# New order lists for tiles 3 to 8 of a fused attention and ReGLU kernel, with six of eight corner clears per tile on GpSimd

## The chip, the cores and the metric

The kernel runs on one core of a Trainium2 chip. The metric is device time in microseconds (us) of one execution, the median of several runs. A core has a matrix engine (TensorE, PE in the profile, with its weight loads as PEld), and VectorE (DVE), ScalarE (ACT), GpSimd (POOL) and SyncE (SP). Each has its own list of instructions and executes it in order; between engines, semaphores make a reader wait for its writer. DMA transfers are issued from the lists of SP, ACT and POOL. SBUF is the on-chip memory; PSUM holds matmul results in eight banks.

## The reference

The kernel must compute block-causal attention, and then a gated feed-forward layer on its output:

```python
# q, k, v: (8 batches, 8 heads, 576 rows, 64), block = 64
scores = scale * np.matmul(q, k.transpose(0, 1, 3, 2))
mask = block_i >= block_j
attn = softmax(np.where(mask, scores, -1e9))
attn_out = np.matmul(attn, v)
x = attn_out.transpose(0, 2, 1, 3).reshape(8 * 576, 512)
# w_gate, w_val: (512, 1536), w_out: (1536, 512)
gate = np.maximum(x @ w_gate, 0.0)
val = x @ w_val
out = gate * val @ w_out          # (4608, 512), float32
```

## The kernel before

**Tiles.** The 4608 output rows are made in nine tiles of 512. Tile j, for j from 0 to 7, holds the first 512 rows of batch j; tile 8 holds the last 64 rows of all eight batches. While the feed-forward layer of tile j is computed, the attention of batch j+1 runs in its gaps, and q, k and v of batch j+2 are loaded. So tiles 0 to 6 carry attention work, and tiles 7 and 8 do not.

**Two ways of ordering.** All engines run under a manual schedule: the order in which the program calls the operations is the order of each engine's list. Tiles 0 to 2 come from a generator of feed-forward steps (`ffn_gen`), between which actions of the attention are called when a count of steps reaches their due time (the table `AT`). Tiles 3 to 8 come from `program(j)`, which executes a written list of tokens one by one: `ORDER_3_6` for tiles 3, 4, 5 and 6, `ORDER_7` and `ORDER_8` for the last two.

**Tokens of the attention.** (The next batch is `up`.)
- `A` followed by a digit: a visit, the score matmuls of 128 query rows (L611). `E1s`, `E1f`, `E1t`, `E1u`: its four exponentials on ACT (L616, L623). `K` and `k`: the last 64 keys (L640) and their exponential (L649).
- `C` and two digits: the corners. The exponentials of a visit also fill blocks that the mask excludes; they are set to zero (L1526 on DVE, L1529 on POOL) before the products read them.
- `V`: products of the probabilities with v for half of the heads (L759, L773), into one PSUM bank. `N`: division by the row sums (reciprocal L696, products L698 and L705, on DVE).
- `T`: the result of a visit is transposed to `xT` by a DMA that SP issues (L842), the input of the next tile's feed-forward layer.
- `l` and `w`: loads of q and k, and of v, issued by POOL (L489). `d0` to `d3`: DMA transposes of q, k and their tails, issued by SP (L499, L504, L506).

**Tokens of the feed-forward layer.** The hidden dimension is cut into 12 chunks of 128. Chunks 0, 1, 8 and 9 of tiles 3 to 6 are computed plainly: `g` and `v` are the matmuls (L1322), `r` the relu on ACT (L1317), `h` the product of the gate and the value (L1445, DVE). The other chunks go in pairs (pairs 1, 2, 3 and 5 in tiles 3 to 6, all six in tiles 7 and 8), each by Strassen's method: seven products of half-size blocks in place of eight. `p15` is product 5 of pair 1 (L1348). The parts of a pair are joined by copies on ACT (`a` L1371, `b` L1374, `l` L1389) and additions (`s` L1377, `m` L1382, `y` L1393, `z` L1396), and `H` and `L` (L1401, L1415) multiply them with the relu and write the hidden activations `hT`. The output product is done by seven products too: `M` and a digit, six tokens each (L1033), whose operands are sums of `hT` blocks (`s` and four digits, L992); tokens `o` add the results (L1080, with ACT's copies L1085, L1092 and L1095) and `S` stores them (L886 for tile 8). `X` and `Y` are sums of `xT` blocks (L1154), `P` is the last store of the previous tile, and `U` (in tile 6 only) are sums of weight blocks that tiles 7 and 8 need (L950).

**Banks and engines.** Several tables go with the lists: `SLOTS` says which of the buffers of a kind each new tile of that kind takes (the PSUM banks `sc` and `ffnp`, and the SBUF buffers `ob` and `gate_sb`), `PAIR_BANK` and `AV_BANK` which banks a pair's products and the products `V` use, and `ON_POOL` which tokens run on POOL instead of DVE. A token that is named with its tile and in `ON_POOL` runs on POOL, such as `31H` for `p1H` in tile 3. A buffer comes free when its last reader has finished. So the position of a token in the list decides both when an engine gets to it and how long its bank is held.

The corner tokens do this (L1476 to L1482):

```python
elif k == "C":
    i, c = map(int, of)
    corners(
        4 * up + i,
        zero_pool if f"{i}C" in ON_POOL else zero_dve,
        (((0, 512),), ((896, 128),))[c],
    )
```

No name of that form is in `ON_POOL`, so all eight clears of tiles 3 to 6 run on DVE. The line in the changed kernel differs, as the diff shows.

Of the kernel before, what the change touches and what calls it, by code (L numbers as in the profile page):

```python
# [17 lines left out]
def kernel(  # L18
# [27 lines left out]
            "010101010101010010101010101010101010101010101010101010101001110010100110"  # L46
            "100111001010011010011100101001101001110010100110100110100101"
# [3 lines left out]
            "201021102101020120120120121201202101202101202101210210201102220201101202"  # L51
            "001201202112000202112102022102102011022202011012020012012021120002021121"
            "0202210210122001201200121012012"
        ),
        "ob": (
            "043210432104310420312142324014203124304232410421302431423240142031243042"
            "324104210324103140231403"
# [5 lines left out]
    }  # L63
    ORDER_3_6 = """
        A0 E0t X1 X3 X4 X6 Y4 g0 X7 E0u E0s C01 E0f g0 K g0*2 r0 k g1*2 v0*2 C00 l0 l1
        l2 v0 p15 v0 h0 p15 p1a g1*2 V00 U02 N00 r1 P V01 N01 p12*2 p1b p1s p13 l3 w0
        p13 p1r p11 v1*2 p11 l4 l5 p1m p14 p16*2 p1y d0 p14 p1l v1 U01 U06 U42 l6 l7 l8
        d1 d2 A1 E1u v1 h1 p17*2 p32 E1t E1s E1f p25*2 p32 g8 p1z p1L C11 p22*2 g8*2
        p35*2 C10 s0101 p1H s0112 p2a p23*2 p2b p24 p21 g8 p21 p24 p3b p2r p26 s0012 l9
        l10 d3 w1 p3a p3s s0001 p26 p2s p2m p2y p2H p33*2 p31*2 p3m p2l p27*2 p2z p3r  # L70
        p36*2 p3y r8 p34*2 p3l V11 N11 A2 E2t E2u E2f p2L p37*2 p3z U41 w2 w3 p52*2
        s1101 p55*2 s0212 p3L p5b v8*2 V10 N10 p51 v8*2 h8 p5a p53*2 p51 p54 p5s p5m E2s
        C21 g9*2 p54 s1201 p5r p56 g9 p56 g9 p5l p57 r9 p57 v9*4 p5y p5z C20 h9 M3*2 A3
        E3t p5L s2001 E3s p3H U45 s1012 s2101 s1112 s1001 E3u p5H s2112 U05 E3f U07
        s2012 V21 N21 C31 M4 M3*2 M4 M3*2 U46 U47 w4 w5 C30 V20 N20 M1*3 M4*3 T1 T0 oa
        M5 M1*2 M4 ob V31 M5 V30 M5 N31 M5*2 T2 N30 T3 M1 M5 M2*4 oy M2*2 S0 oz s0201
        s2212 s1212 S1 s2201 M6*2 om M7 M6*3 oc od M7 M6 M7*4 o6 S2 o7
    """
    ORDER_7 = """
        p15 p05 X1 p05 p0a p02*2 p0b p12*2 p1b p01 X3 X4 p03 p0s p03 p0r p15 p1a p04*2  # L80
        p0l p01 p1s X6 p06*2 p13*2 p1r p25*2 X7 p07*2 p0m p0y p0H Y1 p0z p0L p11 p22*2
        p11 P p2a p2b p2s p23*2 p2r p16 p14*2 p1l p16 p1m p1y p24 p26 p21*2 p26 s0101
        p24 p2l p1H p35*2 p3a p2m p2y p32*2 p27*2 p45 p3b p3s p45 p4a s0001 p2H p2z
        p17*2 p1z p33 p34 p33 p55 p42*2 p3r p34 p31*2 p2L p4b p4s p1L p3l p36*2 p55 p5a
        p3m p3y p3H s1101 p43*2 p4r p44 p37*2 p3z p3L s0112 p52 p41 p46 p52 p5b p41 p4m
        p53*2 p5r p5s p51 p44 p4l p51 p46 p4y p54 p47 p56 p54 p4H p5m p56 p5y p5l M4 p47
        p4z p57*2 p5z M3 M4 M3 M1 p5H M4*4 p4L p5L s1012 s1112 M3 s2112 s2101 M3*3 oa
        s0012 s1001 M1*5 M5 s2001 M5 s2012 M5*4 oy S0 ob M2*5 s0212 s0201 M6 s1201 s2212
        M2 M7 s1212 M6 s2201 oz S1 M6 M7 M6*3 om oc od o6 Y3 M7*4 o7 S2
    """  # L90
    ORDER_8 = """
        X6 p12*2 p1b p15*2 p1a p1s X7 p02*2 p0b p05*2 p14 p11*2 p13*2 p0a p0s p1m p01
        p03 p14 p01 p0m p03 p1r p16*2 p1y p1H p1l p17*2 p1z p0r p06*2 p04*2 P p0y p22*2
        p1L p0l p0H p2b s0112 p25*2 p32*2 p35 p07 p35 p2a p2s p07 p0z p0L p23*2 p3a p24
        p21*2 p2m p24 p2r p26*2 p3b p3s p2y p2H p55 p2l p33*2 p31 p34 p31 p34 p3r p36
        s0001 p3m p36 p3y p3H p55 p27*2 s0101 p2z p3l p37*2 p3z p52*2 p51 p5a p42 p45*2
        p5b p54 p53*2 p2L p3L p5s p42 s1001 p41 p4a p43 p41 p51 p43 p5r p56 p5m p56 p54
        p5y p4b p4s p44*2 p4m p5H p4r M3 p46*2 p5l p57 p4l p47*2 p57 M3 p4y p4z p5z M4*2
        p4H M4*3 p4L p5L M1 M4 M3*3 s1012 s1101 s2101 M3 s1112 M1 s2112 M1*3 oa s0012 M5
        s2001 M5 s2012 M5*4 ob oy S0 s2212 M2*5 M1 s0212 s2201 M2 oz S1 s1212 s0201  # L100
        s1201 M6*6 om oc o6 M7*6 S2 od o7b Sb o7a Sa
# [39 lines left out]
        (7, 0): ('one', 'sc', 'sc'),  # L141
        (7, 1): ('ffn', 'ffn', 'one'),
        (7, 2): ('ffn', 'sc', 'sc'),
        (7, 3): ('one', 'ffn', 'ffn'),
        (7, 4): ('sc', 'ffn', 'one'),
        (7, 5): ('sc', 'ffn', 'ffn'),
        (8, 0): ('sc', 'ffn', 'ffn'),
        (8, 1): ('ffn', 'one', 'sc'),
        (8, 2): ('sc', 'ffn', 'one'),
# [6 lines left out]
        2oc 2od 31H 32H 33H 33s 35H 35s 3od 41H 42H 43H 43s 45H 45s 4od 51H 52H  # L156
        53H 53s 55H 55s 5od 61H 62H 63H 63s 65H 65s 6od 70H 71H 71s 72s 73H 73s
        74H 74s 75H 75s 7od 81H 82H 82s 83H 83s 84H 84s 85H U02 U06 U07 U41 U42
        U45 U46 U47
# [10 lines left out]
    AV_BANK = {0: ('sc', 'one'), 1: ('ffn', 'ffn'), 2: ('sc', 'ffn'), 3: ('ffn', 'sc')}  # L170
    U_AT = {'U15': 300, 'U12': 306, 'U11': 312, 'U16': 386, 'U17': 389, 'U25': 320, 'U22': 326, 'U21': 332, 'U26': 392, 'U27': 395, 'U35': 340, 'U32': 346, 'U31': 352, 'U36': 398, 'U37': 401, 'U55': 360, 'U52': 366, 'U51': 372, 'U56': 404, 'U57': 407}
# [1135 lines left out]
    def program(j):  # L1307
# [128 lines left out]
        def do(t):  # L1436
# [38 lines left out]
            elif k == "C":  # L1475
# [3 lines left out]
                    zero_pool if f"{i}C" in ON_POOL else zero_dve,  # L1479
# [51 lines left out]
    with tc.manual_schedule(engines={E.PE, E.DVE, E.Activation, E.Pool, E.SP}):  # L1531
# [45 lines left out]
        place = [0]  # L1577
# [36 lines left out]
        def mains_1(hp):  # L1614
# [8 lines left out]
        AT = {  # L1623
            "p00": -41,
            "p02": -40.5,
            "cq4": -40,
            "cq6": -39.5,
            "M1q": -39,
            "M1k": -38.5,
            "p01": -38,  # L1630
            "c0": -37.5,
            "j3": -37,
            "p11": -36.5,
            "M2q": -36,
            "p10": -35.5,
            "M2k": -35,
            "p12": -34.5,
            "j2": -34,
            "M3q": -33.5,
            "M3k": -33,  # L1640
            "cv0": -32.5,
            "cv2": -32,
            "c1": -31.5,
            "p20": -31,
            "a0": -30.5,
            "p21": -30,
            "b0": -29.5,
            "p22": -29,
            "a1": -28.5,
            "b1": -28,  # L1650
            "p31": -27.5,
            "x0": -27,
            "cv00/01": -26.5,
            "cv00/23": -26,
            "cg00/01": -25.5,
            "p30": -25,
            "cv4a": -24.5,
            "cv4b": -24,
            "cg00/23": -23.5,
            "x1": -23,  # L1660
            "p32": -22.5,
            "c2": -22,
            "c3a": -21.5,
            "c3b": -21,
            "cv6a": -20.5,
            "a2": 3,
            "b2": 3.01,
            "cv6b": 3.02,
            "C1": 3.03,
            "a3": 6,  # L1670
            "b3": 6.01,
            "x2": 6.02,
            "x3": 8,
            "g01": -53.5,
            "v01": -53.4,
            "g10": -49.5,
            "v10": -49.4,
            "g11": -49.3,
            "v11": -49.2,
            "g20": -0.39,  # L1680
            "v20": -0.38,
            "g21": 7.2,
# [392 lines left out]
```

## Time and profile before

| | |
|---|---|
| median of 3 runs | 348.46 us (348.35 to 348.99) |
| profiled execution | 348.39 us |
| its span, and what lies around it | 346.6 us, 1.79 us |
| PE busy | 334.8 us, 97% |
| DVE busy | 273.0 us, 79% |
| ACT busy | 207.5 us, 60% |
| POOL busy | 194.7 us, 56% |
| tiles 3 to 6 | about 36 us each, from 140 to 284 |
| tile 7, tile 8 with the tail | 27 us, 35.6 us |

Busy time is the time in which an engine executes, as a share of the span. PE and PEld overlap, since weights are loaded while the previous product runs. A time of a row is its start, counted from the start of the span. A note such as `[0.27 <-ACT gate_sb L1317]` at the end of a row says how long the engine was idle before it, and which instruction released it. The windows are stretches of the span, with each engine's busy time in them and the number of its instructions.

### The profile page before, as it was taken

The page shows a single profiled execution, that of the slowest core. Times are in us where ns is not written, and L with a number is a line of the kernel's source. Part 1 is how long each engine was busy: PE and PEld are TensorE (multiplying, and loading weights), DVE is VectorE, ACT ScalarE, POOL GpSimd, SP SyncE. Part 2 cuts the span into 40 slices and gives each one's busy share as a digit, 9 for nine tenths or more (in the row PEclk, how much of TensorE's full clock was granted, in tenths as well). Part 3 has the DMA queues.
Part 4 walks back from the last instruction along what each step waited for, and adds up shares of the span by engine and source line. Part 5 has one row for each costly group of instructions (what it writes and reads, how often), then busy time and mean ns, then how long its engine had stood idle before and what let it go on. Part 6 is the DMA issues. An engine that isn't in the chain of part 4 may idle for free.

```text
span 346.6 us, 9051 instructions
## 1 busy us (share of the span) xinstructions
PE 334.8 (97%) x3481; PEld 233.9 (67%) x3518; DVE 273.0 (79%) x690; ACT 207.5 (60%) x341; POOL 194.7 (56%) x229
## 2 busy tenths in 40 slices
PE   8999999999999999999999999999999999999994
PEld 4544455545545559676977787778778788888873
DVE  4854455768629897789977997899899989999995
ACT  4942756587335872687468746884588537526721
POOL 2767566477795901986087627872155636612530
PEclk9999999999999999999999999999999999999999
DMA  8999999999999994999299929993400141012005
GB/s 244 294 352 373 360 217 242 229 155 176 184 218 113 137 191 82 190 174 139 40 158 181 152 40 156 164 171 47 121 32 2 33 129 33 2 41 83 3 0 121
DMA packets 155403, 50.07 MB, mean 144 GB/s; under 512 B 134464, under 2 KB 151744, under 8 KB 155360
## 3 DMA queue, kind: packets, MB, share of 16 engines
q1 hardware_dynamic: 77520, 32.52, 43.7%
q0 software_dynamic: 70528, 8.98, 43.3%
q10 hardware_dynamic: 7312, 8.00, 8.3%
q8 instruction: 27, 0.44, 0.5%
q14 instruction: 16, 0.13, 0.1%
HBM read 37.75 MB, written 9.44 MB: 136 GB/s over the span
## 4 chain that ended last, share of the span: by engine, by line
PE 75%; DMA 10%; DVE 9%; issue 2%; ACT 2%; POOL 1%; DVEq 0%; SPq 0%; ACTq 0%; POOLq 0%
PE ffnp L1033 11%; PE ffnp L1162 11%; PE ffnp L1348 9%; PE ffnp L1322 7%; PE sc L1348 7%; PE ffnp L1265 5%; PE one L1348 5%; PE one L1033 4%; PE sc L611 3%; DMA stage<-in_moe_w_out_dram 3%; PE ffnp L759 3%; DMA stage<-in_moe_w_val_dram 2%; DMA stage<-in_moe_w_gate_dram 2%; PE one L611 2%; DVE ob L1382 2%
## 5 line engine op out<-in xcount | busy, mean ns | idle before, releaser
L616 ACT ACTIVATE attnT<-sc 128x1024 bf16<-128x1024 f32 x56 | 56.3, 1037 | 0.0
L1033 PEld LDWEIGHTS <-stage 128*128 128x128 bf16 x420 | 39.9, 98 | 4.8 <-DVE stage L992 0.2
L992 DVE TENSOR_TENSOR stage<-hT 128x512 bf16<-128x512 bf16 (+2 forms) x120 | 39.6, 382 | 0.2
L1162 PE MATMUL ffnp<-xT,wg 128*128 128x512 bf16 x130 | 36.2, 379 | 0.6
L1172 ACT ACTIVATE gate_sb<-ffnp 128x512 bf16<-128x512 f32 x35 | 20.5, 598 | 27.0 <-PE ffnp L1162 22.7
L1080 POOL TENSOR_TENSOR ob<-ob,ob 128x512 f32<-128x512 f32 x7 | 8.9, 1268 | 45.7 <-DVE ob L1080 19.9
L1348 PEld LDWEIGHTS <-stage 128*128 128x128 bf16 x288 | 27.6, 98 | 7.4 <-issue 0.4
L759 PEld LDWEIGHTS <-attnT 128*128 128x128 bf16 x640 | 26.1, 98 | 9.2 <-DVE attnT L1526 1.1
L1033 PE MATMUL ffnp<-stage 128*128 128x256 bf16 x252 | 32.0, 273 | 0.0
L1162 PE MATMUL ffnp<-xT,wv 128*128 128x512 bf16 x108 | 31.3, 380 | 0.2
L1182 DVE TENSOR_TENSOR hT<-gate_sb,ffnp 128x512 bf16<-128x512 bf16 x28 | 19.1, 684 | 14.1 <-PE ffnp L1162 11.5
L623 ACT ACTIVATE attnT<-one 128x512 bf16<-128x512 f32 (+1 forms) x28 | 15.0, 536 | 22.2 <-PE ffnp L611 11.6
L489 POOL DMA_DIRECT2D v_bf<-in_v_dram x30 | 24.5, 826 | 3.5 <-PE sc L759 1.6
L1348 PEld LDWEIGHTS <-wg 128*128 128x128 bf16 x224 | 21.5, 98 | 5.7 <-issue 1.5
L1348 PEld LDWEIGHTS <-wv 128*128 128x128 bf16 x224 | 21.8, 98 | 4.1 <-DVE perm L1154 0.2
L1265 PE MATMUL ffnp<-wo,hT 128*128 128x512 bf16 x91 | 23.2, 379 | 0.3
L1162 PEld LDWEIGHTS <-wv 128*128 128x128 bf16 x144 | 12.9, 98 | 14.7 <-issue 1.8
L1162 PEld LDWEIGHTS <-wg 128*128 128x128 bf16 x144 | 13.4, 98 | 13.8 <-issue 0.5
L1401 POOL TENSOR_TENSOR hT<-gate_sb,ob 128x512 bf16<-128x512 bf16 x16 | 19.0, 1188 | 4.0 <-DVE ob L1393 3.9
L489 POOL DMA_DIRECT2D q_bf<-in_q_dram x20 | 18.0, 906 | 3.7 <-DVE recip L732 3.5
L611 PEld LDWEIGHTS <-kTm 64*128 64x128 bf16 x384 | 11.3, 94 | 12.9 <-issue 7.3
L1377 POOL TENSOR_TENSOR ob<-ob,ob 128x512 f32<-128x512 f32 x8 | 10.1, 1265 | 16.7 <-ACT ob L1371 10.2
(228 smaller groups left out, 911.7 us busy)
## 6 DMA issues: line engine op xcount, KB each, us to landing
out_dram<-ob ACTq DMA_DIRECT2D x28, 256.0 KB, 3.6
stage<-in_moe_w_val_dram SPq DMA_DIRECT2D x6, 512.0 KB, 8.7
stage<-in_moe_w_gate_dram SPq DMA_DIRECT2D x6, 512.0 KB, 8.3
stage<-in_moe_w_out_dram SPq DMA_DIRECT2D x6, 512.0 KB, 10.5
q_bf<-in_q_dram POOLq DMA_DIRECT2D x20, 128.0 KB, 4.8
k_bf<-in_k_dram POOLq DMA_DIRECT2D x20, 128.0 KB, 5.9
v_bf<-in_v_dram POOLq DMA_DIRECT2D x20, 128.0 KB, 6.3
stage<-in_v_dram SPq DMA_DIRECT2D x19, 128.0 KB, 5.4
```

What stands on the lines that cost most here:

```text
L489: ins = nc.gpsimd.dma_start(dst, part_of)
L611: nc.tensor.matmul(o, kTm[b % 2][head_of(hh), c, hp, :], qT, start=True, stop=True)
L616: return lambda: nc.scalar.activation(at[:, :, lo : lo + 512], sc, AF.Exp, scale=scale)
L759: nc.tensor.matmul(av[:, p, :], at[:, col : col + 128], v_bf[b % 2][:, c, h, :], start=(p == 0), stop=(c == p), skip_group_check=True,)
L992: nc.vector.tensor_tensor(out=out.rearrange("p (c n) -> p c n", c=m), in0=a, in1=b, op=op)
L1033: nc.tensor.matmul(to, sums.of(c)[which][:, 128 * p : 128 * p + 128], right, start=first, stop=(c == 5), skip_group_check=True,)
L1162: nc.tensor.matmul(to, (wg, wv)[t][f // 4][:, c, 128 * (f % 4) : 128 * (f % 4) + 128], x[:, c], start=(c == 0), stop=(c == 3),)
L1172: nc.scalar.activation(gate_sb, gate, AF.Relu)
L1182: nc.vector.tensor_tensor(out=h, in0=gate_sb, in1=val, op=AX.mult)
L1265: nc.tensor.matmul(op, hT[f][:, 128 * s : 128 * (s + 1)], wo[f // 4][:, f % 4, n0:n1], start=(f == 0), stop=(f == 11),)
L1322: nc.tensor.matmul(to, (wg, wv)[t][f // 4][:, c, 128 * (f % 4) : 128 * (f % 4) + 128], x[:, c], start=(c == 0), stop=(c == 3),)
L1348: nc.tensor.matmul(st[key][:, 256 * k : 256 * k + 256], left[:, c, 128 * k : 128 * k + 128], right[:, c], start=new and (k, c) == (0, 0), ...
```

## The change

The three lists are replaced, and with them the tables of buffers. In tiles 3 to 6 six of the eight corner clears are put on POOL, and the two others stay on DVE; the token that picks the engine now asks for the tile and the corner. `U42`, `U46` and `U47` move from POOL to DVE and `U05` from DVE to POOL; `80s` (the addition s of pair 0 in tile 8) moves to POOL. The products V of visit 0 swap their banks, and those of visit 3 take `sc` twice. The due times of tiles 0 to 2 become a written list; it gives each engine the instructions of those tiles in the same order as before. Number and kind of the matmuls stay as they are.

```diff
     ORDER_3_6 = """
-        A0 E0t X1 X3 X4 X6 Y4 g0 X7 E0u E0s C01 E0f g0 K g0*2 r0 k g1*2 v0*2 C00 l0 l1
-        l2 v0 p15 v0 h0 p15 p1a g1*2 V00 U02 N00 r1 P V01 N01 p12*2 p1b p1s p13 l3 w0
-        p13 p1r p11 v1*2 p11 l4 l5 p1m p14 p16*2 p1y d0 p14 p1l v1 U01 U06 U42 l6 l7 l8
-        d1 d2 A1 E1u v1 h1 p17*2 p32 E1t E1s E1f p25*2 p32 g8 p1z p1L C11 p22*2 g8*2
...
-        s2012 V21 N21 C31 M4 M3*2 M4 M3*2 U46 U47 w4 w5 C30 V20 N20 M1*3 M4*3 T1 T0 oa
-        M5 M1*2 M4 ob V31 M5 V30 M5 N31 M5*2 T2 N30 T3 M1 M5 M2*4 oy M2*2 S0 oz s0201
-        s2212 s1212 S1 s2201 M6*2 om M7 M6*3 oc od M7 M6 M7*4 o6 S2 o7
+        X1 l0 A0 E0u l1 w0 E0s E0f C00 X3 g0*3 X4 X6 X7 Y4 v0*3 p15 g0 g1 p15 g1 E0t v0
+        r0 h0 K k g1 C01 V01 N01 V00 p12*2 p1a N00 w1 w2 P p13*2 v1 p11*2 l2 g1 v1 U02
+        U06 w3 p1b p1r l3 p16 p14 p1s p1m U41 p16 l4 p1y p1H r1 p14 p1l v1 A1 E1u U42
+        p17*2 p1z p21*2 E1t v1 p25*2 h1 E1s C11 p32*2 E1f p1L p2a p22 U01 s0101 s0012
+        p3b p22 p2b g8 s0112 s0001 p2s l5 l6 C10 p35*2 p3a g8 p23 g8 p23 p2r p3s p34
...
+        p36 p3y V11 N11 A2 E2t E2u p2L p37*2 p3z E2f p52 p55*2 p5a p52 p5b U45 V10 v8*2
+        l7 l8 d0 d1 l9 l10 s1101 s1201 s0212 p3L N10 E2s C20 p5s C21 T1 d2 p51 p53*2 p5r
...
+        s2212 s2112 s0201 N21 M4 V20 M4*2 M1*5 s2001 w5 E3s C31 C30 N20 T2 d3 T0 V30 V31
+        oa ob M2 s1001 s1012 M2*3 M5 M6 s1212 N30 N31 T3 M5 M2*2 M5 M6 om s2201 M5*2 oz
+        M5 M7 oy S1 S0 U47 M6 U07 M7 M6*3 M7*4 oc U46 o6 od o7 S2
     """
     ORDER_7 = """
...
-        p53*2 p5r p5s p51 p44 p4l p51 p46 p4y p54 p47 p56 p54 p4H p5m p56 p5y p5l M4 p47
-        p4z p57*2 p5z M3 M4 M3 M1 p5H M4*4 p4L p5L s1012 s1112 M3 s2112 s2101 M3*3 oa
...
+        p46 p41 p44 p4l p41 p4m p4y p4H p53 p54 p53 p5r p54 p51 p47 p56 p47 p56 p5m p5y
+        p4z M4 p5l p57 M4 p57 p5z M3*2 p5H M4 p4L s1112 M4*3 M1*2 p5L M3 s1001 M3*3
...
     ORDER_8 = """
...
-        p5y p4b p4s p44*2 p4m p5H p4r M3 p46*2 p5l p57 p4l p47*2 p57 M3 p4y p4z p5z M4*2
-        p4H M4*3 p4L p5L M1 M4 M3*3 s1012 s1101 s2101 M3 s1112 M1 s2112 M1*3 oa s0012 M5
...
-        s1201 M6*6 om oc o6 M7*6 S2 od o7b Sb o7a Sa
...
+        s1101 p41 p54 p5l p5m p5y p5H s1112 M3 p4m p46*2 p4y p57*2 p5z p4l p47*2 p4z
+        M1*2 p4H M4*6 p5L p4L M3*5 oa s0001 s2101 s2112 M1*4 s1012 s1001 M5 s2001 s2012
...
+        M7*3 M6 M7 M6 oc od o7b Sb o7a Sa M6*2 o6 S2
     """
@@
-        (7, 0): ('one', 'sc', 'sc'),
+        (7, 0): ('sc', 'ffn', 'sc'),
...
     ON_POOL = set(
         """
-        2oc 2od 31H 32H 33H 33s 35H 35s 3od 41H 42H 43H 43s 45H 45s 4od 51H 52H
...
-        74H 74s 75H 75s 7od 81H 82H 82s 83H 83s 84H 84s 85H U02 U06 U07 U41 U42
-        U45 U46 U47
+        2oc 2od 31H 32H 33H 33s 35H 35s 3C00 3C01 3C11 3C21 3C30 3C31 3od 41H
...
+        6C01 6C11 6C21 6C30 6C31 6od 70H 71H 71s 72s 73H 73s 74H 74s 75H 75s 7od
+        80s 81H 82H 82s 83H 83s 84H 84s 85H U02 U05 U06 U07 U41 U45
         """.split()
     )
@@
-    AV_BANK = {0: ('sc', 'one'), 1: ('ffn', 'ffn'), 2: ('sc', 'ffn'), 3: ('ffn', 'sc')}
+    AV_BANK = {0: ('one', 'sc'), 1: ('ffn', 'ffn'), 2: ('sc', 'ffn'), 3: ('sc', 'sc')}
@@
-                    zero_pool if f"{i}C" in ON_POOL else zero_dve,
+                    zero_pool if f"{j}C{of}" in ON_POOL else zero_dve,
@@
-        for n in sorted(acts, key=lambda n: AT[n]):
-            at = int(AT[n])
-            ffn(at - place[0])
-            place[0] = max(place[0], at)
-            acts[n]()
+        for item in ORDER_0:
+            t, _, times = item.partition("*")
+            if t == "f":
+                ffn(int(times or 1))
+            else:
+                acts[t]()
```

346 lines of the change are left out of this document (59 added, 287 removed).

## The prediction

> **What bounds the kernel now.** I read the page first, then the windows by tile, then the waits of PE, then the timelines at the places where PE waits.
>
> ```profile
> PE 334.8 (97%) x3481; PEld 233.9 (67%) x3518; DVE 273.0 (79%) x690; ACT 207.5 (60%) x341; POOL 194.7 (56%) x229
> PE 75%; DMA 10%; DVE 9%; issue 2%; ACT 2%; POOL 1%; DVEq 0%; SPq 0%; ACTq 0%; POOLq 0%
> ```
>
> TensorE is busy for 97% of the span and carries the chain. The DMA share of that chain lies in the first tiles, which the change leaves alone. The windows are the tiles 3, 4, 5, 6, then 7, then 8 with the tail:
>
> ```profile
> 140.00:176.00 36.00, 35.51 (x416) 27.64 (x416) 31.74 (x83) 24.13 (x41) 22.73 (x26) 1.00 1.33 138
> 176.00:212.00 36.00, 35.62 (x414) 27.48 (x416) 31.05 (x83) 23.93 (x41) 21.84 (x25) 1.00 1.25 136
> 248.00:284.00 36.00, 35.64 (x409) 28.00 (x408) 32.81 (x86) 24.02 (x40) 17.86 (x15) 1.00 0.18 47
> 284.00:311.00 27.00, 26.46 (x236) 22.44 (x235) 25.89 (x54) 14.56 (x27) 12.71 (x10) 1.00 0.09 31
> 311.00:346.60 35.60, 29.87 (x266) 25.28 (x263) 30.05 (x59) 14.99 (x27) 11.82 (x10) 0.99 0.20 53
> ```
>
> After the length come PE, weight loads, DVE, ACT, POOL. PE idles 0.4 to 0.5 us in each 36 us tile; DVE is busy for 31 to 33 of 36, POOL for 18 to 23. The clock granted is full (1.00). So only PE's pauses, and what follows its last matmul, can be won; all the rest is a matmul count that stays.
>
> ```profile
> PE one L1033 <- POOL hT L1401: 0.6, 1, 0.6
> PE sc L611 <- DVE ob L1393: 0.3, 1, 0.3
> PE ffnp L1348 <- ACT q_bf L1389: 0.2, 1, 0.2
> ```
>
> This list shows only long waits. The shorter ones I took from the starts of successive matmuls: where PE streams, rows of 512 columns start 216 ns apart and of 256 columns 109. What exceeds that, leaving out jumps where a record is missing, is a pause. They come to 0.44 us in tile 3 (at 147.3), 0.60 in tile 4 (183.3, 192.3 and a small one), 0.31 in tile 5 (219.5), 0.40 in tile 6 (255.5): 1.75 in all. Tile 7 has 1.5 (294 to 305), tile 8 1.7, of which 0.81 stands at 332.1. Together 5 us is the most that lists can win before the tail. The pause that returns in each of tiles 3 to 6 looks like this:
>
> ```profile
> 179.21 0.69 DVE L1445 TENSOR_TENSOR hT<-gate_sb,ffnp 128x512 bf16<-128x512 bf16 x1 [0.27 <-ACT gate_sb L1317]
> 179.91 0.20 DVE L696 RECIPROCAL recip<-sc 128x5 f32<-128x5 f32 x1
> 181.43 0.69 DVE L1377 TENSOR_TENSOR ob<-ob,ob 128x512 f32<-128x512 f32 x1
> 182.23 0.69 DVE L1382 TENSOR_TENSOR ob<-sc,ob 128x512 f32<-128x512 f32 x1
> 183.12 0.69 DVE L1393 TENSOR_TENSOR ob<-sc,ob 128x512 f32<-128x512 f32 x1 [0.20 <-PE ffnp L1348]
> 183.34 0.92 PE L611 MATMUL sc<-qTm,kTm 64*128 64x512 bf16 x6
> ```
>
> DVE goes from the plain chunk's product (L1445) through two normalisations (L696, L698, L705) to s, m and y of pair 1 (L1377, L1382, L1393). The last one empties a bank `sc` that visit A1 (L611) wants; it ends at 183.81, 3.90 us after the normalisations began, and PE was there at 183.48.
>
> **The change, part by part.** *Tiles 0 to 2* get a written list in place of due times; every engine keeps its instructions in the same order. Cost 0.
>
> *The corners.* Six of eight clears per tile go from DVE to POOL, in tiles 3 to 6.
>
> ```profile
> L1526 DVE MEMSET attnT<- x62: 165/165/165, 9.1 to 276.5; 64x128 uint32 x62
> L1529 POOL MEMSET attnT<- x2: 307/307/307, 129.2 to 129.5; 64x256 bf16 x2
> ```
>
> DVE loses 6 x 0.165 = 0.99 us a tile, POOL gains 6 x 0.307 = 1.84 (from 22.7 to about 24.6 of 36). Neither total bounds a tile, so the exchange is worth only what it moves in the chain above. There it takes no step out: that chain holds no clear. Where a corner could be late is C00 and C01, which now stand behind three DMA issues of POOL (l0, l1, w0: 0.90 each) and before V01. Counting along PE's list, on a scale of its own, the issues end at 168.6, the exp of that block at 169.07, the clears at 169.5, and the matmul of V01 that reads them is due at 169.59. A margin of 0.1: I cost it at 0, between -0.1 and +0.4 per tile.
>
> *Tiles 3 to 6, the pause at A1.* V01 now comes before V00 and their results stand 0.22 us earlier, but the chain still starts behind L1445, which waits for the relu r0 (L1317) at the same place. I count a start 0.10 earlier and the same consumer: 0.31 becomes 0.13 to 0.23. New is the exp of the last keys (k, L649): its bank `one` is reused 0.2 us after the exp can begin, worth 0.05 to 0.10. Visit A2 waits for z of pair 1 (L1396), whose last product is 0.43 later: 0 to 0.10. In all about 0.3 per tile (0.2 to 0.45), 1.2 for four against 1.75: -0.55.
>
> *Loads and transposes.* The value loads move forward, the key loads back, and SP issues d0 and d1 (transposes of q and k, L499) between them, with T1, d2, T2, d3, T0, T3 after, where before all four d went ahead.
>
> ```profile
> 184.12 4.96 SPq L499 DMA_TRANSPOSE qTm<-q_bf  x1
> 189.46 3.09 SPq L499 DMA_TRANSPOSE kTm<-k_bf  x1
> 192.63 1.37 SPq L504 DMA_TRANSPOSE qTt<-q_bt  x1
> 196.25 12.45 SPq L842 DMA_TRANSPOSE xT<-xnat  x4
> ```
>
> On the clock of tile 4: the last key load leaves POOL at about 192.2 to 193.1 (before: 184.1) and lands 5.5 to 6.2 later, 198.6 to 199.3. The transpose of k then holds SP for 3.1 to 3.9 us, five small ones 1.2 each, so T3 leaves at 207.7 to 209.2 and lands 2.4 to 2.7 later: 210.1 to 211.9, middle 211.0. Before, T3 landed 2.2 us ahead of its first sum (173.97 against 176.14 in tile 3, so 210 against 212.1 here) and 2.9 ahead of the first matmul on it. It is about 1 us later and still in time: 0, with 0 to +1 per tile for tiles 4 to 6 at the far end. The cover is that 1.1 us.
>
> *Sums U.* Two tokens go from POOL to DVE, in tile 6 (1.16 against 0.42 us). DVE gains 0.84 there, less the 0.99 of the corners: 0.
>
> *Tile 7.* The last quarter before the output products is pair 5: its product, y (0.69, DVE), H (1.17, POOL, L1401), then M4. In the old list eight tokens lie between, 1.85 us, in the new six and a part, 1.42. This pause grows by 0.4, while the three for low copies (L1389) and hT around 300 to 304, 0.9 together, have more tokens ahead of them. I count 1.3 against 1.5: -0.2 (-0.7 to +0.4).
>
> *Tile 8.* The wait of 0.81 at 332.1 is POOL's H of pair 4 (L1401, 331.78 to 332.94) in front of M4. The new list gives it 0.22 more ahead, leaving about 0.3 at M4 and 0.5 before it at pairs 4 and 5; the early pauses (0.22, 0.30, 0.08) I no longer find. 0.9 against 1.7: -0.8 (-1.2 to +0.2).
>
> *Tail.* Before, the last matmul ends at 341.72, the last half additions at 342.73, the last halves land at 345.36. Now o6 (one addition of 0.69) is last, about 1.05 us after PE, and its store S2 goes by SP and POOL. In the trace S2's POOL half landed 2.9 us after its addition, so 3.95 us after PE against 3.64: +0.3 (0 to +0.6).
>
> *Pauses that I didn't find.* In the new lists I followed only the waits with a margin below 0.3 us; before has two pauses of 0.1 that this would miss. For six tiles +0.3 (0 to +1.2).
>
> Sum: -0.55 - 0.2 - 0.8 + 0.3 + 0.3 = -0.95. The profiled execution took 348.39 us (span 346.6 and 1.79 around it), 0.07 under the median of 348.46, so the forecast is 348.46 - 0.95 = 347.5, or a little less if the two clears of DVE relief arrive where DVE is late: I say 347.4. Its own range is 346.5 to 348.3.
>
> [...] First the rows: POOL's products (L1401, two SBUF inputs) take 1150 to 1339 ns with a median of 1166 although DVE is busy for 88% of these windows, and DVE's additions take 0.69 whether both inputs lie in SBUF or one in PSUM. [...]
>
> **The rivals.** *Slower: SP's queue.* One mechanism: the transpose of k waits for the late key loads and T3 for it. If it takes 5 us, as q's did (4.96; 4.4 in the median), T3 lands at 212 to 213.8 on the clock above, and the first matmul of the next tile, due at 212.9, waits up to 0.9, the first sum 0 to 1.7. It decides once T3 is over 1.1 us later than I put it. At 1 us in each of tiles 4, 5 and 6, with the other gains kept halfway: 348.46 + 3 - 0.5 = 351.0. For it: the key loads move 9 us back. Against: five of five transposes of k took 2.8 to 3.9.
>
> *No change: corners late on POOL.* If C01 waits for one DVE operation, or POOL's issues take 0.1 longer each, V01 stalls 0.2 to 0.4 and with it the whole chain to A1: 4 x 0.25 = +1.0, and 348.4.
>
> *More gain: the freed DVE removes the waits for `sc`.* If the time taken from DVE arrives in the chain to A1, all 1.75 goes and not 0.55: 347.4 - 1.2 = 346.2. Against: DVE waits for PE in that chain, not PE for a full DVE.
>
> **How the numbers follow.** 0.2% is 0.70 us, about what a measurement of this kernel can tell from no change: the bounds are 347.76 and 349.16. My forecast has 0.50 (0.40 below 347.76, 0.10 above), more gain 0.10, corners late 0.17 (all within), SP's queue 0.16, an unseen wait elsewhere 0.07 (slower). Faster 0.50 + a rest of 0.02 from late corners that cost less = 0.52; same 0.10 + 0.15 = 0.25; slower 0.23. For 8 in 10 I leave out half of more gain below 346.2 and the upper half of the slower cases, above 350.2.
>
> **What would show it.** In the changed profile: L1529 with 26 rows and DVE down by about 1 us in each window of 36 us; the pause before L611 `sc` behind L1393 still there, at 0.1 to 0.3; T3 landing about 1 us ahead of the first sum; no wait of 0.6 on hT in tile 8; a store of POOL as the last to land, 3.9 us behind the last matmul. The prediction is wrong if PE waits at a tile's start for xT (first rival), at V01 for the clear (second), or if tiles 7 and 8 pause as long as before.

## The result, and the profile after

The changed kernel takes 349.67 us (median of 7 runs, 349.21 to 349.89), the kernel before in the same comparison 348.38 (7 runs, 348.19 to 348.99). The ratio is 1.0034, with a 95% interval of 1.0022 to 1.0046: slower by a third of a percent. The forecast was 347.4, so its sign was wrong, and the time lies above its own range of 346.5 to 348.3; only the wider span that took in the rivals, 346.2 to 350.2, holds it.

The page of the changed kernel, the engines' busy time and the chain by engine:

```profile
PE 335.3 (97%) x3481; PEld 233.7 (67%) x3518; DVE 267.7 (77%) x667; ACT 206.1 (59%) x341; POOL 202.0 (58%) x252
PE 73%; DVE 11%; issue 6%; ACT 5%; DMA 3%; POOL 1%; POOLq 0%; DVEq 0%; ACTq 0%
```

DVE fell by 5.3 us and POOL rose by 7.3. In number (DVE 23 operations fewer, POOL 23 more) that is what the moved clears and sums ask for; at their lengths they make about 3.8 and 6.3 us of it. In the chain DVE, ACT and "issue" (an engine that waits for nothing that the profile shows) have grown from 13% to 22%. The windows of tiles 3, 4, 6, 7, and 8 with the tail:

```profile
140.00:176.00 36.00, 35.25 (x400) 27.25 (x400) 29.97 (x76) 23.92 (x40) 24.02 (x31) 1.00 1.19 133
176.00:212.00 36.00, 35.64 (x413) 27.52 (x416) 30.14 (x77) 23.85 (x40) 24.13 (x31) 1.00 1.17 123
248.00:284.00 36.00, 35.65 (x414) 27.52 (x416) 32.57 (x82) 23.86 (x40) 17.20 (x20) 1.00 0.20 50
284.00:311.00 27.00, 26.42 (x238) 22.79 (x236) 25.95 (x54) 14.23 (x27) 13.10 (x11) 1.00 0.11 37
311.00:347.40 36.40, 30.73 (x274) 26.24 (x271) 29.76 (x59) 14.94 (x28) 12.85 (x11) 0.98 0.22 59
```

DVE has lost 1.8 and 0.9 us in tiles 3 and 4, and PE did not get it: in the window of tile 3 PE is busy for 0.26 us less than before. The long waits of PE from 130 us on:

```profile
PE one L1056 <- POOL hT L1424: 0.7, 2, 0.5
PE sc L634 <- DVE ob L1416: 0.5, 1, 0.5
```

(Lines 489 and up of the kernel before stand 23 further down here: L1416 is L1393 before, the sum y.) The wait for y in front of visit A1, which was to shrink, is longer in tile 3. As windows cut tiles at round times, I measured each tile from the last matmul of an output product to the next, in all profiles (us; the tail is from PE's last end to the end of the span):

| | tile 3 | 4 | 5 | 6 | 7 | 8 | tail |
|---|---|---|---|---|---|---|---|
| before | 36.03 | 36.19 | 35.92 | 35.93 | 29.03 | 29.25 | 4.86 |
| after | 36.81 | 36.17 | 36.11 | 36.12 | 28.76 | 28.71 | 5.36 |
| the same again (e1) | 36.81 | 36.38 | 36.28 | 36.12 | 28.75 | 28.72 | 5.37 |

In the profiled execution of after (349.21 us, the fastest of its seven runs) the differences add up to +0.78 - 0.02 + 0.19 + 0.19 - 0.27 - 0.54 + 0.50 = +0.83, which is the growth of the span from 346.58 to 347.42. The rest up to the 1.29 between the medians lies in tiles 4 and 5, which vary from one execution to the next, as the second row shows.

So tiles 7 and 8 gained, the tail lost, and tiles 3 to 6, which were to gain 0.55, lost 1.1 or more. The experiments ask which part of the lists does that.

### The profile page after: what moved, and what is told of

It is laid out like the page before. It is cut to its first block, busy times and chain, and to the rows that moved or that the text cites. A ratio compares the mean times of both kernels' runs of the same rounds, so it can differ in the third digit from the quotient of the medians.

```text
span 347.4 us, 9062 instructions
## 1 busy us (share of the span) xinstructions
PE 335.3 (97%) x3481; PEld 233.7 (67%) x3518; DVE 267.7 (77%) x667; ACT 206.1 (59%) x341; POOL 202.0 (58%) x252
## 4 chain that ended last, share of the span: by engine, by line
PE 73%; DVE 11%; issue 6%; ACT 5%; DMA 3%; POOL 1%; POOLq 0%; DVEq 0%; ACTq 0%
PE ffnp L1185 15%; PE ffnp L1056 11%; PE ffnp L1371 7%; PE sc L1371 6%; PE ffnp L1288 6%; PE one L1056 4%; PE ffnp L1345 4%; PE sc L634 3%; PE one L1371 2%; PE ffnp L782 2%; DVE ob L1405 2%; PE one L634 2%; PE sc L782 2%; PE one L1185 2%; ACT attnT L639 1%
## 5 line engine op out<-in xcount | busy, mean ns | idle before, releaser
L1015 DVE TENSOR_TENSOR stage<-hT 128x512 bf16<-128x512 bf16 (+2 forms) x120 | 40.3, 386 | 0.2
L1195 ACT ACTIVATE gate_sb<-ffnp 128x512 bf16<-128x512 f32 x35 | 20.5, 599 | 27.4 <-PE ffnp L1185 22.9
L1103 POOL TENSOR_TENSOR ob<-ob,ob 128x512 f32<-128x512 f32 x7 | 8.9, 1266 | 38.6 <-ACT ob L1115 23.2
L646 ACT ACTIVATE attnT<-one 128x512 bf16<-128x512 f32 (+1 forms) x28 | 15.1, 539 | 13.3 <-PE ffnp L634 12.9
L1340 ACT ACTIVATE gate_sb<-ffnp 128x512 bf16<-128x512 f32 x24 | 14.7, 613 | 12.2 <-PE ffnp L1345 5.0
L1552 POOL MEMSET attnT<- 64x256 bf16 x26 | 7.6, 306 | 23.2 <-ACT attnT L639 19.5
```

The source lines that it names most:

```text
L1015: nc.vector.tensor_tensor(out=out.rearrange("p (c n) -> p c n", c=m), in0=a, in1=b, op=op)
L1195: nc.scalar.activation(gate_sb, gate, AF.Relu)
```

## The experiments

**The halves of the change.** First the changed kernel once more, to see what of it repeats.

> The changed kernel as it is, for a second profile. In the first, tile 3 ended 0.78 us later against before than it began, tiles 5 and 6 lost 0.19 each, tiles 7 and 8 won 0.27 and 0.54, and the part behind the last matmul grew by 0.50. Theory A (the lists): the same pauses at the same places, within 0.1 us each, tile 3 among them. Theory B (accident of one execution, such as the 0.32 and 0.40 us that ACT's copy b and DVE's y waited in tile 3 for nothing that the profile shows): tile 3's loss moves or goes, by 0.4 us or more.

One execution took 349.44 us; its tiles are in the table. Tile 3 repeats to 0.01 us, tile 4 does not (36.17 and 36.38).

Then the new lists of tiles 3 to 6 with the old ones of 7 and 8, and the other way round:

```diff
 # e3_new_3_6: the changed kernel, but
-    ORDER_7, ORDER_8, PAIR_BANK of 7 and 8, 80s, the ends of SLOTS: as after
+    ORDER_7, ORDER_8, PAIR_BANK of 7 and 8, 80s, the ends of SLOTS: as before
 # e4_new_7_8: the kernel before, but
+    ORDER_7, ORDER_8, PAIR_BANK of 7 and 8, 80s, the ends of SLOTS: as after
```

> The new list, banks and corners for tiles 3 to 6, with the old lists and banks for tiles 7 and 8. Theory A: the loss of tiles 3 to 6 alone, +1.1 us by the profile, up to +1.6: 349.5 to 350.0. Rival D (the loss comes from tiles 7 and 8 with the tail): within 0.3 of before.

> The old list, banks and corners for tiles 3 to 6, the new lists and banks for tiles 7 and 8. Theory A: -0.8 from the two tiles and +0.5 from the tail, so 348.0 to 348.2, a ratio of 0.9985 to 0.9995. Rival D: slower than before by 0.5 us or more.

e3 took 354.32 us, 1.0158 [1.0142, 1.0175]; e4 349.18, 1.0019 [1.0010, 1.0027]. Neither number is the worth of its half, because each has a seam. `SLOTS` hands out buffers by number, and where one list follows on another, a tile can get a number whose last store has not left yet. In e3's tile 7, the wait of PE and the windows around it (length, PE, PEld, DVE, ACT, POOL, clock, DMA share, GB/s):

```profile
PE one L1370 <- ACT ob L1393: 3.1, 1, 3.1
284.80:290.00 5.20, 2.10 (x21) 1.73 (x19) 1.78 (x5) 0.76 (x2) 0.07 (x1) 1.00 0.33 107
290.00:294.20 4.20, 4.20 (x26) 2.97 (x25) 3.00 (x6) 2.87 (x6) 2.14 (x2) 0.61 0.00 0
294.20:300.00 5.80, 5.80 (x54) 5.14 (x53) 4.77 (x9) 3.92 (x7) 2.85 (x4) 0.98 0.14 47
```

ACT waits for the `ob` buffer, PE for ACT, for 3.1 us, and behind the pause the granted clock is 0.61 in the mean of a window of 4.2 us. (The trace shows 1.00 until 290.96, then 0.50 for 3.41 us, then 1.00 again.) Tile 7 takes 33.73, 4.7 more than before: 3.1 of waiting and 4.2 x 0.39 = 1.6 of slow clock. (Lines of the experiments stand one or two off those of after.) In e4 a pause of the same kind, 0.8 us, stands before the product that starts at 286.42, and its tile 7 takes 29.83. What the halves do show lies away from the seam: e3's tiles 3 to 6 are those of after (36.81, 36.51, 36.12, 36.11), and e4's tile 8 is 28.72. The loss is in the lists of tiles 3 to 6, with their buffers, banks and clears.

**The corners.** In the changed kernel, all clears back on DVE:

```diff
 # e2_corners_dve: the changed kernel, but
-    ON_POOL: ... 3C00 3C01 3C11 3C21 3C30 3C31 ... 6C31
+    ON_POOL: no C names
```

> The changed kernel with all eight corner clears back on DVE, lists and banks as changed. Theory A (the order of tiles 3 to 6 and the tail cost the time): within 0.4 us of the changed kernel, so 349.3 to 350.0, a ratio to before of 1.0025 to 1.0045. Rival C (the clears on POOL cost it: late at V01, or POOL and DVE hindering each other): back to 348.0 to 348.6, a ratio of 0.999 to 1.001.

And in the kernel before, the same six names put on POOL, with its own lists:

```diff
 # e5_corners_pool: the kernel before, but
+    ON_POOL: 3C00 3C01 3C11 3C21 3C30 3C31 ... 6C31
-    zero_pool if f"{i}C" in ON_POOL else zero_dve,
+    zero_pool if f"{j}C{of}" in ON_POOL else zero_dve,
```

> The old lists and banks, with only the six corner clears per tile of tiles 3 to 6 put on POOL. If the prediction's reading holds that the exchange of engines is worth only what it moves at the pause before A1, and nothing stands ahead of the clears on POOL: -0.4 to +0.2 us, 348.0 to 348.6. Rival C (POOL's clears come late or hinder DVE): slower by 0.7 us or more.

e2 took 357.02, 1.0245 [1.0228, 1.0261], over 7 us more than after; e5 368.77, 1.0574 [1.0555, 1.0594], 20 us more than before. PE's largest wait of e2, then its V01 in tile 3:

```profile
PE sc L780 <- DVE attnT L1547: 5.8, 4, 1.7
```

```profile
144.72 0.33 PE L780 MATMUL sc<-v_bf,attnT 128*128 128x65 bf16 x5 [1.29 <-DVE attnT L1547]
```

The clear waits on DVE behind the sums of `xT` and the product of chunk 0, and V01 waits for it, once in each of four tiles. In e5, PE's two largest waits, then POOL's timeline at that place:

```profile
PE ffnp L1349 <- DVE ob L1383: 9.7, 4, 3.6
PE sc L760 <- POOL attnT L1530: 2.4, 1, 2.4
```

```profile
142.06 0.31 POOL L1530 MEMSET attnT<- 64x256 bf16 x1 [1.74 <-ACT attnT L617]
142.91 0.31 POOL L1530 MEMSET attnT<- 64x256 bf16 x1 [0.55 <-ACT attnT L617]
143.42 3.57 POOL L490 DMA_DIRECT2D q_bf<-in_q_dram  x4 [0.20 <-issue]
146.95 0.92 POOL L490 DMA_DIRECT2D v_bf<-in_v_dram  x1
147.82 0.73 POOL L490 DMA_DIRECT2D q_bt<-in_q_dram  x1
148.50 3.56 POOL L490 DMA_DIRECT2D k_bf<-in_k_dram  x4
151.96 0.42 POOL L1530 MEMSET attnT<- 64x256 bf16 x1
152.46 1.15 POOL L1402 TENSOR_TENSOR hT<-gate_sb,ob 128x512 bf16<-128x512 bf16 x1
```

In the old list the clears C00 and C01 stand ahead of ten DMA issues in a row. POOL works its list in order, so it waits 1.74 and 0.55 us for ACT's exponentials before it can clear, and the ten issues start at 143.42, where before they started at 140.06. Behind them, and behind C11, stands H of pair 1 (L1402), at 152.46 and not at 148.66 (POOL's L1401 in the kernel before). DVE's sum waits 1.80 us for this H, and PE for what DVE does next (m, L1383): the 9.7 us in four tiles. The 2.4 is a clear that is late in tile 6. The four tiles take 20.5 us more than before. Of this the two waits are 12.1, and three stretches at half clock behind the pauses (3.41, 3.41 and 6.83 us) make an estimated 6.8.

So the engine of a clear and its place in the list are one decision. In the changed kernel both fit: its clears C00 and C01 run on POOL from 142.80 to 143.36, V01 starts at 143.18, its sixth matmul, the first that reads the second of them, at 143.41 with a pause of 0.08 us, and nobody is listed as waiting for the clears on POOL. Their group, and that of the clears left on DVE:

```profile
L1552 POOL MEMSET attnT<- x26: 306/306/308, 129.2 to 276.8; 64x256 bf16 x26
L1549 DVE MEMSET attnT<- x38: 165/165/165, 9.0 to 269.6; 64x128 uint32 x38
```

**Tile 3.** It loses most, 0.78, and repeats. The chain of after between 145.24 and 149.04, with start and length:

```profile
145.24 0.58 ACT ob L1397
145.82 0.51 ACT gate_sb L1340
146.33 0.04 issue
146.37 0.38 PE sc L1371 x2
146.75 0.22 PE ffnp L1371 x2
146.97 0.22 PE sc L1371 x2
147.19 0.23 PE ffnp L1371 x2
147.42 0.03 issue
147.45 0.05 DVEq L1416
147.50 0.40 issue
147.90 0.70 DVE ob L1416
148.60 0.04 issue
148.65 0.39 PE sc L634 x4
```

DVE's y is free to start at 147.50, all its waits done, and starts at 147.90. Nothing in the trace holds it. ACT's copy b (L1397) shows the same, 0.32 us between its last wait and its start at 145.24. What b loses goes down the chain: ACT's relu (L1340) follows b, PE's next product of pair 1 waits for the relu (a pause of 0.23 at 146.37), y waits for the last of these products, and A1 (L634) for y. In seven profiles with this list the delay of y is 0.396 to 0.414 us. Is it the list? First, tile 3 with its old list:

```diff
 # e8_old_3: the changed kernel, but
-        3: ORDER_3_6,
+        3: ORDER_3,        # the list of before, with its AV_BANK, clears on DVE
```

> The changed kernel with tile 3 alone in the old order (old list, banks of V, and corners on DVE in that tile), tiles 4 to 8 as changed; buffers that tile 4 takes over are renamed to the order in which tile 3 frees them. If the 0.78 us that tile 3 lost in both profiles is that tile's own: 0.6 to 0.9 us faster than the changed kernel, 348.8 to 349.1. If it is a cost that the boundary to tile 2 or the loads bring in any order: no change, 349.7.

The median was 349.37, 1.0029 [1.0017, 1.0041]; tile 3 fell to 36.02. The median is above the 349.1 that I had as its upper bound: tiles 4 and 5 took 36.41 and 36.25 in its profile, and tile 8 took 29.07. So the new list, with its buffers and clears, brings the loss of tile 3 about. Next, a suspicion that the buffer which b and y write was the cause:

```diff
 # e10_swap_ob: the changed kernel, but from tile 3 on
-    SLOTS["ob"] = ... 4310421031340...
+    SLOTS["ob"] = ... 4301420130341...   (0 and 1 exchanged)
```

> The changed kernel with the buffers ob0 and ob1 exchanged from tile 3 on, the lists unchanged. In tile 3 of every profile of the new list ACT's copy b starts 0.45 us, and DVE's y of pair 1 0.50 us, after the last instruction that each needs, both with ob1 as output. If that buffer holds them: b and y start at once, product 1 of pair 1 and visit A1 lose their waits of 0.23 and 0.64, and tile 3 takes 36.1 to 36.3 us. If the place in the list does it: 36.8 as before.

One execution took 349.67; tile 3 was 36.45. b started at once, y was late by 0.41 as ever. A buffer that held both would not let go of one alone. What had changed for b was its number: with the exchange ACT had one semaphore row fewer ahead of it. Counted along the rows of the trace (instructions and semaphore rows of one engine, from 0), the late b was row 191 and the late y row 319; with the exchange b is row 190. In the kernel before, DVE's row 447, the semaphore row ahead of a y in tile 4, starts 0.40 late too. The numbers are 128 or a multiple of it apart. A packet of 8192 bytes on the queue that the page lists as `q14 instruction` begins within 0.4 us of y's late start in all seven profiles. So I shifted the numbers and left the lists alone:

```diff
 # e12_pad: the changed kernel, but at the end of tile 2
+            for n in range(18):
+                nc.vector.memset(pads[:, n % 10 : n % 10 + 1], 0.0)
+            for n in range(4):
+                nc.scalar.copy(pads[:, 10 + n : 11 + n], zeros[:, n : n + 1])
```

> The changed kernel, with eighteen memsets of 128 x 1 on DVE and four copies of 128 x 1 on ACT put into the end of tile 2, where DVE idles 2.1 us (136.72 to 138.81) and ACT 2.4 (137.38 to 139.75). They write a tile that nobody reads; all the computation is there, and no list of tiles 3 to 8 is touched. What is to be explained: in tile 3 of the changed kernel DVE's y of pair 1 (L1416) starts 0.40 us after its last wait is done (0.402 to 0.414 in seven profiles), and ACT's b (L1397) 0.32 us, with no releaser in the trace. Counted along each engine's rows in the trace, semaphore rows among them and the first being 0, y is row 319 of DVE and b row 191 of ACT, and a packet of 8192 bytes on the queue that brings instructions lies at 147.8. Theory A: each engine pauses at every 128th row while its next instructions come, whatever the instruction is. Then the pause moves: DVE's to the X sums at 140.8 to 142.1, which have 0.5 us of idle time behind them, ACT's to the rows before 143.5, and b and y of pair 1 start within 0.1 us of their last wait. Tile 3 falls from 36.81 to between 36.0 and 36.4, the median to 348.9 to 349.4 (349.67 before less 0.3 to 0.8). The next place, row 447, then falls 18 rows earlier, to the sums of hT (L1015) of tile 4 at about 188. Theory B: the new list holds b and y in itself (a bank, a port, a neighbour on another engine). Then y starts 0.40 and b 0.3 us late as before, tile 3 stays at 36.7 to 36.9, and the median at 349.4 to 349.9.

Both delays are gone. DVE around y, and the same stretch of the chain (lines stand one further down here):

```profile
145.80 0.69 DVE L1401 TENSOR_TENSOR ob<-ob,ob 128x512 f32<-128x512 f32 x1 [0.18 <-ACT ob L1398]
146.60 0.69 DVE L1406 TENSOR_TENSOR ob<-sc,ob 128x512 f32<-128x512 f32 x1
147.49 0.69 DVE L1417 TENSOR_TENSOR ob<-sc,ob 128x512 f32<-128x512 f32 x1 [0.20 <-PE ffnp L1372]
```

```profile
147.19 0.23 PE ffnp L1372 x2
147.43 0.02 DVEq L1417
147.45 0.04 issue
147.49 0.70 DVE ob L1417
```

y starts 0.04 us after its wait, b (145.19) also 0.04. The pause at A1 is 0.22 in place of 0.64, and tile 3 takes 36.24. So theory B of this run falls: with no token of tile 3 moved, the delays went. Of theory A, that much is shown: the delay hangs on how many rows the engine has behind it. That it happens at *every* 128th row is not: here the X sums that are now at row 319 run back to back, and DVE's idle time after them, 0.67 us before the product of chunk 0, was as long in after. In the kernel before, row 319 is the semaphore row just ahead of y in tile 3, and it starts on time.

What happens at such a row stays open. For a link with that queue speaks a count that I had not made: each of the 14 profiles has exactly 16 packets of 8192 bytes on it within its span, and DVE, ACT, POOL and SP together have exactly 16 rows whose number is 63 above a multiple of 128 (7, 4, 3 and 2), as 191, 319 and 447 are. Against a plain wait for these bytes speaks the order in time: the packet near y ends 0.20 to 0.43 us after y has begun, and the packet nearest to b begins 2.3 to 2.7 us after b. So the cause at the row is not shown, and the count of rows is.

The median of e12 was 349.46 (11 runs: ten from 348.83 to 350.63, one of 356.17), 1.0028 [1.0013, 1.0043], against 1.0034 of after; its fastest run, the profiled one, is 0.38 below the fastest of after. The gain of 0.57 in tile 3 is plain in the profile; the medians do not show it. Tile 2 ends at 139.34 there, 0.23 later than in after, which lies within what the other profiles show (138.96 to 139.69, e7 aside), so that the padding costs this is not shown.

**Tile 4.** Its length in five profiles with the new list (after, e1, e3, e6, e7) is 36.17, 36.38, 36.51, 36.90, 36.69. First suspicion: SP's queue, the slower rival, so T0 was issued ahead of both d0 and d3:

```diff
 # e7_t0_early: the changed kernel, but
-        l7 l8 d0 d1 ...   ... T2 d3 T0 V30 V31
+        l7 l8 T0 d0 d1 ...   ... T2 d3 V30 V31
```

> The changed kernel with one token moved: T0, whose data are there early in the tile, goes ahead of d0 on SP instead of standing between d3 and T3. The first rival (SP's queue makes T3 late): T3 leaves 1.2 us earlier, PE's waits for xT at the start of tiles 4 and 5 (0.23 us at 214.4 and 0.14 at 177.8 in the second profile of the changed kernel, none in the first) go, and the median falls by 0.2 to 0.5 us, to 349.2 to 349.5, with executions closer together. If T3 has time enough: no change, 349.7.

The median was 349.89, 1.0043 [1.0007, 1.0078], with three of ten runs above 352; in the profiled execution tiles 0 to 2 took 3 us longer, but tile 4, with 36.69, was no shorter. So the order of T0 is not the cause. ACT's timeline at the start of tile 4 in the slowest case (e6, below), and in after:

```profile
173.98 0.58 ACT L1115 COPY ob<-ffnp 128x512 f32<-128x512 f32 x1 [0.52 <-PE ffnp L1056]
174.59 2.53 ACTq L896 DMA_DIRECT2D out_dram<-ob  x2
177.17 0.60 ACT L646 ACTIVATE attnT<-ffnp 128x512 bf16<-128x512 f32 x1 [2.61 <-DVE ob L1103]
```

```profile
174.10 0.58 ACT L1115 COPY ob<-ffnp 128x512 f32<-128x512 f32 x1 [0.52 <-PE ffnp L1056]
174.18 2.28 ACTq L896 DMA_DIRECT2D out_dram<-ob  x3
176.56 0.60 ACT L646 ACTIVATE attnT<-ffnp 128x512 bf16<-128x512 f32 x1 [1.88 <-PE ffnp L634]
```

Between the copy and the first exponential of the new tile (E0u, L646) ACT issues the store S2 of the tile before (L896). This one issue takes 0.38, 0.64, 0.78, 1.17 and 0.97 us in after, e1, e3, e6 and e7; E0u starts 0.65, 0.85, 0.99, 1.38 and 1.17 us after the last output product, and PE pauses 0, 0.14, 0.28, 0.66 and 0.46 us before p15, which needs the bank that E0u reads. Two more profiles fit: in e10 the issue takes 0.99, E0u starts after 1.19, PE pauses 0.48 and the tile takes 36.71; in e12 the issue takes 0.38, PE does not pause and the tile takes 36.11. (The 36.41 of e8 has another cause: its issue takes 0.38, and PE waits 0.3 us for DVE elsewhere.) The old list has ten plain matmuls (g0, g1, v0) between A0 and p15, the new one six, 1.3 us of cover. With that issue on SP:

```diff
 # e9_s2_sp: the changed kernel, but
+            last = 3 <= j <= 6 and (hi, n0) == (1, 256)
-            (nc.sync if j == 2 else nc.scalar).dma_start(
+            (nc.sync if j == 2 or last else nc.scalar).dma_start(
```

> The changed kernel with the store S2 of tiles 3 to 6 issued by SP instead of ACT. In six profiles with the new list the issue of S2 on ACT at the start of tile 4 took 0.38, 0.64, 0.78, 0.97 or 1.17 us, the exponential queued behind it came as much later, and PE then waited 0, 0.14, 0.28, 0.46 or 0.66 us for the bank of product 5 of pair 1. If that queue is the cause: in tile 4 no such wait, the first exponential before 0.5 us after the last output product of tile 3 (now 0.65 to 1.38), tile 4 at 36.0 to 36.2, and the median 0.2 to 0.5 us lower than the changed kernel, 349.2 to 349.5. If the wait belongs to something else that is late there (xT): it stays, and the median too, 349.7.

Tiles 4 to 6 were 36.17, 36.11 and 36.11, with no pause before p15. The median, 349.30, is 0.37 under after's, but against the kernel before in its own comparison the ratio is 1.0035 [1.0021, 1.0049], no lower than the 1.0034 of after: a gain in time is not shown. In one profile alone the lengths could be luck, as after itself has 36.17; the seven pairs of issue and pause are the stronger evidence, though why the issue takes longer in one execution than in another was not found.

**The tail.** The old last line of tile 8, in the changed kernel:

```diff
 # e6_old_tail: the changed kernel, but
-        M7*3 M6 M7 M6 oc od o7b Sb o7a Sa M6*2 o6 S2
+        M6*4 oc o6 M7*4 S2 od o7b Sb o7a Sa
```

> The changed kernel with the end of tile 8 as before: the last products are M7, after them only the two half additions o7b and o7a with the stores Sb and Sa. If the tail of the changed list costs what the profiles show (5.36 us from the last matmul to the end of the span against 4.86): 0.4 to 0.6 us faster than the changed kernel, 349.0 to 349.3. If that difference is hidden by something else that ends last: no change, 349.7.

The tail fell from 5.36 to 5.15, and not to 4.86: its half additions begin 0.56 us behind PE's last matmul, in the kernel before 0.26. The median, 349.64, 1.0034 [1.0024, 1.0044], shows nothing of 0.2 us, and the profiled execution has the long issue in tile 4 shown above.

**The parts that gained, alone.** The kernel before with the new lists of tiles 7 and 8, their buffers renamed so that the seam of e4 goes, and e6's tail:

```diff
 # e11_seam_tail: e4_new_7_8, but
-    SLOTS["ob"] = ... 324112401342013021304213
+    SLOTS["ob"] = ... 324102410342103120314203
-        M7*3 M6 M7 M6 oc od o7b Sb o7a Sa M6*2 o6 S2
+        M6*4 oc o6 M7*4 S2 od o7b Sb o7a Sa
```

> Tiles 0 to 6 as before; the new lists and banks for tiles 7 and 8 with the buffers renamed at the seam to the order in which tile 6 frees them, and the end of tile 8 as before. If the gains of the new lists for tiles 7 and 8 (0.27 and 0.54 us in the changed kernel) are theirs, and the wait of 0.97 us at the seam came from the names of the buffers: 0.4 to 0.8 us faster than before, 347.6 to 348.0, a ratio of 0.9977 to 0.9988. If they hang on the new list of tile 6: no faster than before, 348.3 to 349.2.

347.74 us (11 runs, 347.51 to 348.02), a ratio of 0.9980 [0.9971, 0.9988] to before: faster than both kernels. Its tiles are 36.02, 36.18, 35.93, 35.91, 28.79, 28.71, its tail 5.15. Its windows of tile 4 and of tiles 7 and 8:

```profile
176.00:212.00 36.00, 35.83 (x418) 27.50 (x414) 31.04 (x83) 23.98 (x40) 21.84 (x25) 1.00 1.38 136
284.00:311.00 27.00, 26.42 (x238) 22.82 (x237) 26.19 (x55) 14.58 (x27) 12.59 (x10) 1.00 0.06 21
311.00:346.20 35.20, 29.69 (x264) 25.30 (x262) 28.70 (x57) 14.59 (x27) 12.86 (x11) 0.98 0.22 61
```

DVE is busier in tile 4 than in the changed kernel (31.04 against 30.14), and the tile is as long in both (36.18 and 36.17): 0.9 us less work on DVE bought nothing there.

e6 and e11 have the same lists for tiles 7 and 8 and the same tail. They part only in tiles 0 to 6, in lists, buffers and clears: 349.64, 1.0034 [1.0024, 1.0044], against 347.74, 0.9980 [0.9971, 0.9988]. So these parts cost 1.9 us, and here the medians show it too.

## Why the prediction was wrong, step by step

- **What bounds the kernel: right.** PE pauses and the tail are all that moved. That less work on DVE bought nothing by itself is seen in tile 4 (e11).
- **"Cost 0" for tiles 0 to 2: right in time.** The end of tile 2 is 139.10 before and 139.11 after. But whether b and y started 0.32 and 0.40 us late or 0.04 (e12) hung on the count of rows that their engines had behind them, and the new lists changed that count in tile 3. The prediction counted no rows, and tile 3, with 0.78, is the largest single loss; 0.57 of it went when the rows were shifted (e12).
- **Tiles 3 to 6, -0.55: wrong, +1.1 to +1.9; this is the step that turned the sign** (sums of the four tiles in after, e1 and e6 against 144.07 before). The step "0.31 becomes 0.13 to 0.23" did come out in tiles 4 to 6 (0.09) and, once the delay was shifted away, in tile 3 (0.22). What failed is "in all about 0.3 per tile". In tile 3 the pauses add up to 1.2 us, 0.64 at A1, 0.23 at pair 1's p11 behind the late b, 0.17 at 140.5 where a bank waits for the last addition of tile 2's output. In tiles 4 to 6 a pause of 0.24 at pair 3 (the bank that m reads, L1405) and one of 0.13 at A3 (z, L1419) replaced what was won at A1; no run took these two away. In tile 4, ACT's issue of S2 added up to 0.7 more in some executions. I had followed waits with a margin below 0.3 only around A1 and A2.
- **Loads and transposes, 0: the landing was mis-sized, and the wrong engine watched.** T3 of tile 3 landed at 177.91, 1.99 us after the tile's end, where before it landed 1.16 ahead of it: 3.1 us later and not 1.0. It left 1.0 later, measured from the tile's end, as put; the rest is the landing, 4.79 us in place of 2.65 and of the 2.4 to 2.7 that I took. The slower rival had a late T3, and its price fell on the wrong engine: DVE's first sum waited, and PE did not, as its first product on T3's part of `xT` comes at 178.2 or later. The last line of the view of the T transposes (L865) of after, and a line from that of the sums (L1177), what ended the idle time of their engine, in us and times:

```profile
DMA to landing us min/median/max: 2.4/3.5/8.4
```

```profile
  DMA xT<-xnat: 1.2, 2
```

  The median landing takes 3.5 us, where before it took 2.7. Two waits of DVE with 1.2 us in sum; a third, 1.03 us at 214.18, the view puts down to a store, though it ends 0.19 after T3 of tile 4 has landed. PE waited for T3 only in e1 (0.23 at tile 5) and e6 (0.14). The queue that did cost PE time was ACT's, with S2's issue before E0u. The prediction listed SP's and POOL's queues and not ACT's.
- **Corners, 0 on a margin of 0.1: right in the number, wrong in the reason.** "Worth only what it moves in the chain" misses that the new places of V and C need the clears off DVE: back there they cost 7.4 us (e2). A clear that is off the chain in one list is on it in the other.
- **Tile 7, -0.2: right** (-0.27; the pause before M4 grew to 0.66 from 0.31, as put).
- **Tile 8, -0.8: right in kind, a third too large** (-0.54). POOL's H still delays M4 by 0.40, where 0.3 was put, and three small pauses of 0.11 to 0.14, which I "no longer found", stand at 323 to 327.
- **Tail, +0.3: under-sized, +0.50.** POOL's half of S2 landed 3.98 us behind PE's last matmul, close to the 3.95 put for it. But SP's half, which I had not followed, was the last, 4.21 behind it, where before the last landing was at 3.64.
- **Second rival, a clear on POOL that waits for an operation of DVE: not shown.** In after the 26 memsets on POOL take 306 to 308 ns, beside a DVE that is busy for 83% of the window of tile 3, and the waits that the trace lists ahead of them are for ACT's exponentials (19.5 us in ten) and none for DVE (3.0 us of "issue" is the rest). The loss lies elsewhere.

The sum: -0.55 became +1.1 to +1.9, -1.0 for tiles 7 and 8 became -0.81, and +0.3 became +0.50; the +0.3 put by for unseen pauses was a quarter of what they cost in tiles 4 to 6 alone (three times 0.41, the two above and 0.04 at K).

## What to carry to other kernels

A list that is good for one engine's load must be followed through every in-order queue at each tile's seam, those that issue DMAs among them: here one store's issue on ACT, 0.38 to 1.17 us long in seven executions, stood in front of the first exponential. Judge such a change per tile, from one fixed point of the work to the next, and keep what gains: the new lists of tiles 7 and 8 alone are worth 0.2%. Where an engine starts late and nothing released it, count its rows, and shift them with a few empty instructions before blaming the list.

## What the hardware showed that I had not expected

- DVE and ACT started an instruction 0.3 to 0.4 us after its last wait, at a row number that repeats from profile to profile: DVE's row 319 in seven profiles (0.396 to 0.414), ACT's row 191 (0.32) wherever b stands there. Eighteen memsets on DVE and four copies on ACT ahead of it took both away (0.04 each), and tile 3 then took 0.57 us less. The late rows 191, 319 and 447 are 128 apart, and 16 packets of 8192 bytes on `q14 instruction` stand beside 16 such rows; but neither b nor y waited for a packet to land, so the cause stays open.
- The issue of the same store on ACT took from 0.38 to 1.17 us in seven executions. In e1, with 0.64, SP was issuing a transpose of `xT`'s tail at that time, which took 2.04 us, where the same one took 1.21 in after (the eight of its kind there 1.17 to 2.03); whether one delays the other was not tried.
- After a pause of PE of 3.1 us the granted clock was 0.50 for 3.41 us (e3), from 1.1 us after PE went on. In e5, by the starts of the matmuls, pauses of 2.8 and 3.3 us were each followed by 0.50 for 3.41 us and one of 3.7 by 6.83 us; one of 2.6 was not followed by it. (e3's is 3.3 by that measure.) So the shortest pause with a slow stretch behind it was 2.8 us, and the longest of these without one 2.6; why the clock drops was not shown.
